# Batch 1's attention inside block 0's second product: local transposes in pairs, two score parts in one run, v spread first

## The chip, the cores and the metric

One NeuronCore of a Trainium2 chip runs the whole kernel. The metric is the device time of one execution in microseconds (us); lower is better. Engines are named as in the profile: PE (TensorE, matmuls and transposes), PEld (its weight loads), DVE (VectorE), ACT (ScalarE), POOL (GpSimd, which also issues DMAs with a cast), SP (SyncE, which issues DMAs and DMA transposes).

## What is computed

Attention of 8 batches with 8 heads (576 tokens, 64 values per head), and then a two-layer MLP over all 4608 tokens. Heads 0 to 3 look at the last 32 positions ("local"), heads 4 to 7 at every 32nd position back ("strided").

```python
scores = scale * np.matmul(q, k.transpose(0, 1, 3, 2))
mask_local = (rel >= 0) & (rel < stride)                      # stride = 32
mask_strided = (rel >= 0) & (pos[None, :] % stride == pos[:, None] % stride)
attn = softmax(np.where(mask, scores, -1e9))                  # first 4 heads local, last 4 strided
x = (attn @ v) as tokens x 512
h = x @ w_in                                                  # 512 -> 2048
out = (h * tanh(softplus(h))) @ w_out                         # 2048 -> 512
```

## The kernel before, in words

The tokens go through the MLP in 9 blocks of 512, and the attention of a batch is woven into the block before it needs it. The program's order on each engine is written by hand: `tc.manual_schedule()` keeps the order in which the Python code issues instructions, and only the waits are added (a reader waits for its writer, a buffer's next user for its last one).

Block 0 is the special one. Its second product, `mlp2` (L773 to L793), is 16 steps; each is four 128x128 by 128x512 matmuls at L781. With `fc_major=True` the steps go through the 16 chunks of w_out in four quarters: steps 0 to 3 read chunks 0 to 3, steps 4 to 7 the second quarter, steps 8 to 11 the third, steps 12 to 15 the last. Each quarter of w_out is a DMA of its own, issued on POOL's queue (L190) between the loads of batch 1's and batch 2's q, k and v. After step i the loop at L1011 runs the list `at[i]`, and these lists hold batch 1's attention. They come from `attn_steps(1, y, y)`, the branch `if x == y` (L455 to L474), in which the attention has one double PSUM bank of its own, `acc(x)`, and two single rotating banks, `tile_t` (tag "pt").

The entries of the lists, with their short names in the code:

- `T[0]` to `T[7]`, `t_step` (L245): transposes of k and q on PE into a rotating bank, and a copy to SBUF. T[0] to T[3] are the strided heads (8 transposes each, L253), T[4] to T[7] the local heads: k and q of head pair 0, then of pair 1 (12 transposes of 96x64 each, L267). The copies go to DVE (None in the list), for T[5] and T[7] to ACT.
- `Q`, `qk` (L311): score matmuls (L333) of a part, 64 rows of the array for each of two heads, into `acc(x)`, and then Exp on ACT (L347). With `"t"` for the bank it takes two rotating banks and does Exp in two instructions (L343). The strided scores have three parts (6, 6 and 4 units of two heads), the local ones too (5, 5, 2).
- `M`, `mask` (L349): a multiplication on DVE (L353).
- `V`, `pv` (L374): four matmuls (L369) into a rotating bank, then a reciprocal (L380) and a product (L381) on DVE into x_s or x_l. The first four strided pv (0 to 3) need the strided parts 0 and 1, the others parts 1 and 2.
- `spread_v_str` (L156): v of the strided heads copied on DVE from the tile in which its DMA put it to the layout that pv reads. The DMA of the next batch's v into that tile waits for it.
- `X`, `xt` (L400): transposes of the result into xT, which the MLP reads, and a copy. `xt("l", hf)` does three windows of 96 tokens of the local heads; `xt_now(n)` does n windows in one rotating bank; `xt_later(n)` leaves the windows from n on to DMA transposes on SP (L445). Later batches use the last two.
- `sums_w()` (L676): sums of quarters of w_out on DVE for the later blocks.

Before, the copies of the transposes and both parts of the first scores alternate with the steps:

```python
T[2:4], [Q(x, s0)],
[M(*s0), Q(x, s1)],
[lambda: spread_v_str(b, nc.vector), V("s", 0)],
[V("s", 1), M(*s1), Q(x, ("s", 2))],
[V("s", 2), T[4]],
[V("s", 3), M("s", 2), T[5]],
[V("s", 4), T[6]],
[V("s", 5), T[7]],
```

At L965 further work is added to the lists: at step 3 the loads of batch 2's v and local k and q on POOL (`load_early_v_str`, `load_tiles_loc`) with a cast of batch 1's local v between them, at step 12 the DMA transposes of batch 2 on SP (L224, L230), at 1, 7, 9 and 11 the sums of w_out. After step 15 block 1 begins: `mlp1(1, ...)` with its products at L553.

Of the kernel before, what the change touches and what calls it, by code (L numbers as in the profile page):

```python
# [11 lines left out]
BF16 = mybir.dt.bfloat16  # L12
# [5 lines left out]
WQ = 96  # L18
CL, PL = 6, 96
# [24 lines left out]
def kernel(ctx, tc, q, k, v, moe_w_in, moe_w_out, out):  # L44
    nc = tc.nc
# [61 lines left out]
    def acc(i, name):  # L107

        pool = ps_z[0] if i == 2 else ps_a
        return pool.tile([128, 2, 512], F32, tag=f"acc{i}", name=name)  # L110
# [23 lines left out]
    def by_head(x):  # L134

        return x[0:PL].rearrange("p j h d -> p (j h d)").rearrange("p (h x) -> p h x", h=4)
# [19 lines left out]
    def spread_v_str(b, eng):  # L156
        cast(eng, vs[b % 2][0:PN, :, :, 0:D], vs_raw().rearrange("p h (j d) -> p h j d", d=D))
# [37 lines left out]
    def cast(eng, out_, in_):  # L195
        if eng is nc.scalar:
            nc.scalar.copy(out_, in_)  # L197
        else:
            eng.tensor_copy(out_, in_)
# [42 lines left out]
            eng.memset(vl[b % 2][0:32, 0, :, 0:D], 0.0)  # L242


    def t_step(b, kind, which, hp, eng=None):  # L245

        eng = eng or nc.vector
        tr = tile_t("tr")[:].bitcast(BF16)
        if kind == "s":
            src = (qs if which == "q" else ks)[b % 2]  # L250
            for u in range(8):
                h, jj = 2 * hp + u // 4, u % 4
                nc.tensor.transpose(  # L253
                    tr[:, PN * u:PN * u + PN],
                    src[0:PN, h, 128 * jj:128 * jj + 128],
                    ident[0:PN, 0:PN],
                )
            dst = (qTs if which == "q" else kTs)[:, 8 * SU * hp:8 * SU * hp + 8 * SU]
            cast(
                eng, dst.rearrange("c (u n) -> c u n", u=8)[:, :, 0:PN],  # L260
                tr[:, 0:S].rearrange("c (u n) -> c u n", u=8),
            )
        else:
            src = by_head((ql if which == "q" else kl)[b % 2])
            for j in range(CL):
                for e in range(2):
                    nc.tensor.transpose(  # L267
                        tr[64 * e:64 * e + 64, PL * j:PL * j + PL],
                        src[:, 2 * hp + e, D * j:D * j + D], ident[0:PL, 0:PL],
                    )  # L270
            dst = qTl[:, hp, :] if which == "q" else kTl[:, hp, 32:32 + S]
            cast(
                eng, dst.rearrange("c (p j) -> c p j", j=CL),
                tr[:, 0:S].rearrange("c (j p) -> c p j", j=CL),
            )

    def unread(n, i_acc=None):

# [15 lines left out]
    class Attn:  # L294
# [129 lines left out]
                    tr[:, 0:576].rearrange("p (j n) -> p n j", j=CS),  # L424
                )

        def xt_now(self, n):
            tr = tile_t("trx")[:].bitcast(BF16)
            t0 = (self.b % RING) * S
            for c in range(2):  # L430
                for w in range(n):
                    o = (n * c + w) * WQ
                    nc.tensor.transpose(
                        tr[:, o:o + WQ], x_l[0:WQ, w, 128 * c:128 * c + 128], ident[0:WQ, 0:WQ]
                    )
            cast(
                nc.scalar, xT[:, 0:2, t0:t0 + n * WQ],
                tr[:, 0:2 * n * WQ].rearrange("p (c n) -> p c n", c=2),
            )

# [6 lines left out]
    def attn_steps(b, x, y):  # L447

        a = Attn(b)
        Q = lambda i_acc, *parts: (lambda: a.qk(parts, i_acc))  # L450
        M = lambda kd, i: (lambda: a.mask(kd, i, nc.vector))
        V = lambda kd, i: (lambda: a.pv(kd, i))
        X = lambda kd, hf: (lambda: a.xt(kd, hf))
        s0, s1, sl2, l0, l1 = ("s", 0), ("s", 1), (("s", 2), ("l", 2)), ("l", 0), ("l", 1)
        if x == y:  # L455
            T = [(lambda n=n, eng=eng: t_step(b, *T_ORDER[n], eng)) for n, eng in enumerate(
                (None, None, None, None, None, nc.scalar, None, nc.scalar))]
            return [
                T[2:4], [Q(x, s0)],
                [M(*s0), Q(x, s1)],  # L460
                [lambda: spread_v_str(b, nc.vector), V("s", 0)],
                [V("s", 1), M(*s1), Q(x, ("s", 2))],
                [V("s", 2), T[4]],
                [V("s", 3), M("s", 2), T[5]],
                [V("s", 4), T[6]],
                [V("s", 5), T[7]],
                [V("s", 6), Q(x, l0)],
                [V("s", 7), M(*l0), Q(x, l1)],
                [X("s", 0), V("l", 0), M(*l1), Q(x, ("l", 2))],
                [X("s", 1), V("l", 1), M("l", 2)],  # L470
                [V("l", 2), V("l", 3)],
                [V("l", 4), V("l", 5)],
                [lambda hf=hf: a.xt("l", hf, nc.vector) for hf in range(2)],
            ], T[0:2]  # L474
        V2 = lambda kd, i, z: (lambda: a.pv2(kd, i, z))
        G = lambda kd, i: (lambda: a.mask(kd, i, nc.gpsimd))
        l2 = ("l", 2)
        now = -(-(512 * (b + 1) - S * b) // WQ)
        at = [
            [],  # L480
            [Q(x, s0), Q(y, s1), Q("t", *sl2), M(*s0), M(*s1), M("s", 2)],
            [],
            [V2("s", 0, y), G(*l2)],
            [],
            [V2("s", 2, y), Q(x, l0), Q("t", l1), G(*l0), G(*l1)],
            [],
            [V2("s", 4, y), lambda: nc.scalar.preload_act_table(AF.Mish)],
            [],
            [V2("s", 6, y)],
            [V2("l", 0, x)],  # L490
            [X("s", 0), V2("l", 2, y), X("s", 1)],
            [V2("l", 4, x), lambda: a.xt_now(now)],
            [lambda: a.xt_later(now)],
        ]
        return at
# [364 lines left out]
    with tc.manual_schedule():  # L860
# [43 lines left out]
        a = Attn(0)  # L904
# [56 lines left out]
        for t in range(NBLK):  # L961
            if t == 0:
                x, y, z = accs
                at, ts = attn_steps(1, y, y)
                at[3] += [  # L965
                    lambda: load_early_v_str(2), lambda: load_tiles_loc(2, kl, k),
                    lambda: cast_v_loc(1, Po), lambda: load_tiles_loc(2, ql, q),
                ]
                at[12].append(lambda: transpose_by_dma(2))
                at[1].append(lambda: sums_w()[0](lo))  # L970
                at[7].append(lambda: sums_w()[0](hi))
                at[9].append(lambda: sums_w()[1](lo))
                at[11].append(lambda: sums_w()[1](hi))
                at[14].append(lambda: sums_x(1, "1"))
                at[15] += [
                    lambda: spread_v_str(2, Dv),
                ]
                out_accs = (z, x)
            else:
                if t == 1:  # L980
                    split_third()
                x, y = 0, 1
                gT, z, g1 = mlp1(t, (y, x) if t == 1 else (x, y))
                at = attn_steps(t + 1, x, y) if t + 1 < B else []
                if t == 1:
                    at[0].append(lambda: sums_w()[3](hi))
                if t + 2 < B:
                    at[10].append(lambda: transpose_by_dma(t + 2))
                if t + 1 < B:
                    at[7].append(lambda: share_v_loc(t + 1))  # L990
                if t + 2 < B:
                    at[0].append(lambda: load_qk_str(t + 2))
                if t + 1 < B:
                    at[12].append(lambda: sums_x(t + 1, "1"))
            for i, g in enumerate(g1):
                g()
                if t == 0:
                    for s in ts if i == len(g1) - 1 else ():
                        s()
                    continue  # L1000
            if t == 0:
                steps = mlp2(t, gT, out_accs, fc_major=True)
            elif t == NBLK - 1:
                mlp2_last(t, gT, z[5])
                break
            else:
                za, zc = [bank(i, "pso")[:].rearrange("p (n o) -> p n o", n=2) for i in range(2)]
                steps = mlp2_seven(t, gT, z[5], za, zc)
                if t + 1 == B:
                    steps[12] = lambda f=steps[12]: (sums_x(t + 1, "1"), f())  # L1010
            for i, g in enumerate(steps):  # L1011
                g()
                if i < len(at):
                    for s in at[i]:
                        s()
                if t > 0 and i == 9 and t + 2 < B:
                    cast_qk_loc(t + 2, Po, Po)
            if t < B - 3:
                load_qk_loc(t + 3)
# [30 lines left out]
```

## Time and profile before

| what | us |
|---|---|
| median of 3 runs | 287.12 (286.89 to 287.18) |
| the profiled execution | 286.68 |
| its span in the profile | 284.8 |
| PE busy | 279.0 (98%) |
| DVE busy | 193.0 (68%) |
| ACT busy | 196.4 (69%) |
| POOL busy | 106.3 (37%) |
| block 0's second product with batch 1's attention, PE | 35.19 to 57.39 |
| block 1, from its first matmul to that of block 2 | 57.39 to 86.44 |

The profile is of one execution, with times from the start of its span. A PE matmul's length includes the way through the pipe, so that neighbours overlap: the pace is read from the starts. Lines of one group (x12) are merged into one row of the order of time. "DMA issues" gives the time from the issue of a DMA to its landing; issue plus that time is when a waiting engine can go on.

### The profile page before, as it was taken

To read this page: it belongs to the slowest core of one execution; us is meant where nothing else is said; L and a number is where in the kernel's file an instruction comes from. 1 tells how busy PE (TensorE), PEld (TensorE's weight loads), DVE (VectorE), ACT (ScalarE), POOL (GpSimd) and SP (SyncE) were. 2 spreads that over 40 slices of the span, in tenths; PEclk is the share of its full clock that TensorE was granted. 3 is DMA by queue.
4 is the path that set the end of the run, shared out by engine and by line. 5 is a ranking of instruction groups with operands and counts; after the bars stand their busy time and mean duration, and the time that the engine had idled before them with its cause. 6 is when DMAs were issued, how large, how long until landed. Compare 5 with 4: busy or idle time off the path is not lost.

```text
span 284.8 us, 7535 instructions
## 1 busy us (share of the span) xinstructions
PE 279.0 (98%) x3121; PEld 218.6 (77%) x3121; DVE 193.0 (68%) x403; ACT 196.4 (69%) x292; POOL 106.3 (37%) x127
## 2 busy tenths in 40 slices
PE   8999999999999999999999999999999999999995
PEld 3564455586898689868988898788978997888684
DVE  2283067899877777777777778777677767644742
ACT  1578652599867987798779877987699759407820
POOL 8375534406290717271636255345404600000000
PEclk9999999999999999999999999999999999999999
DMA  7999999999989999799999999899979041003004
GB/s 155 185 202 195 190 194 201 143 145 235 169 128 129 214 173 150 139 216 158 155 138 217 122 176 136 216 135 153 157 143 164 4 154 30 0 10 140 0 2 147
DMA packets 103965, 40.73 MB, mean 143 GB/s; under 512 B 86396, under 2 KB 99436, under 8 KB 103932
## 3 DMA queue, kind: packets, MB, share of 16 engines
q1 hardware_dynamic: 67900, 25.13, 51.9%
q0 software_dynamic: 35744, 14.87, 46.8%
q8 instruction: 24, 0.39, 0.6%
q10 hardware_dynamic: 288, 0.25, 0.3%
q14 instruction: 9, 0.07, 0.1%
HBM read 37.20 MB, written 9.44 MB: 164 GB/s over the span
## 4 chain that ended last, share of the span: by engine, by line
PE 92%; DMA 2%; DVE 2%; ACT 1%; issue 0%; ACTq 0%; POOLq 0%
PE pso L748 31%; PE psu L553 10%; PE psh L522 10%; PE psv L553 9%; PE psb L553 8%; PE psb L522 5%; PE po L369 4%; PE pso L808 4%; PE pso L781 4%; PE ps L333 4%; DMA ks<-in_k_dram 2%; PE trx L418 1%; PE un L281 1%; PE tr L267 1%; PE tr L253 1%; DVE x_s L395 1%
## 5 line engine op out<-in xcount | busy, mean ns | idle before, releaser
L748 PEld LDWEIGHTS <-gT 128*128 128x128 bf16 x448 | 41.9, 98 | 5.8
L553 PEld LDWEIGHTS <-w_in 128*128 128x128 bf16 x384 | 37.4, 98 | 8.4
L353 POOL TENSOR_TENSOR Pl<-Pl,consts_sb 128x960 bf16<-128x960 bf16 (+1 forms) x18 | 29.2, 1634 | 38.2 <-issue 22.1
L748 PE MATMUL pso<-w_out,gT 128*128 128x256 bf16 x336 | 40.9, 272 | 0.0
L748 PEld LDWEIGHTS <-Sg 128*128 128x128 bf16 x336 | 31.5, 98 | 4.4
L522 PEld LDWEIGHTS <-w_in 128*128 128x128 bf16 x208 | 20.2, 98 | 16.7 <-issue 0.6
L553 PEld LDWEIGHTS <-Sw 128*128 128x128 bf16 x288 | 28.2, 98 | 3.3
L522 PE MATMUL psh<-xT,w_in 128*128 128x512 bf16 (+1 forms) x136 | 29.4, 366 | 0.2 <-ACT xT L197 0.2
L197 ACT COPY xT<-trx 128x576 bf16<-128x576 bf16 (+3 forms) x24 | 14.2, 629 | 18.4 <-PE trx L418 13.0
L748 PE MATMUL pso<-Tw,Sg 128*128 128x256 bf16 x224 | 26.7, 273 | 0.0
L197 ACT COPY osb<-pso 128x512 f32<-128x512 f32 (+1 forms) x17 | 9.4, 555 | 20.2 <-PE pso L748 10.8
L562 ACT ACTIVATE gT<-psu 128x1024 bf16<-128x1024 f32 x16 | 16.4, 1025 | 8.4 <-PE psu L553 8.4
L395 DVE TENSOR_TENSOR x_s<-po,rden 72x512 bf16<-72x512 f32 x28 | 19.2, 686 | 1.0
L656 DVE TENSOR_TENSOR psu<-psb,p 128x512 f32<-128x512 f32 x16 | 11.2, 700 | 11.8 <-PE psb L553 11.0
L533 ACT ACTIVATE gT<-psh 128x1024 bf16<-128x1024 f32 x16 | 16.2, 1024 | 4.0 <-PE psh L522 3.9
L175 POOL DMA_DIRECT2D vl<-in_v_dram x24 | 17.8, 751 | 2.0 <-issue 1.5
L656 DVE TENSOR_TENSOR Sg<-gT 128x256 bf16<-128x256 bf16 (+2 forms) x32 | 12.8, 422 | 8.0 <-ACT gT L562 6.7
L628 POOL COPY mark<-qTl 1x4 bf16<-1x4 bf16 x6 | 1.6, 268 | 44.4 <-DMA qTl<-ql 44.4
L347 ACT ACTIVATE Ps<-ps 72x864 bf16<-72x864 f32 (+1 forms) x18 | 14.7, 857 | 4.6 <-PE ps L333 4.6
L553 PE MATMUL psu<-xT,w_in 128*128 128x256 bf16 x128 | 17.9, 272 | 0.0
L725 DVE TENSOR_TENSOR p<-pso,p 128x512 f32<-128x512 f32 x14 | 9.6, 685 | 11.9 <-PE pso L748 11.9
L553 PE MATMUL psb<-Sx,w_in 128*128 128x256 bf16 x128 | 17.2, 272 | 0.0
(139 smaller groups left out, 612.8 us busy)
## 6 DMA issues: line engine op xcount, KB each, us to landing
out_dram<-osb SPq DMA_DIRECT2D x9, 512.0 KB, 3.9
out_dram<-p SPq DMA_DIRECT2D x7, 512.0 KB, 3.0
kl<-in_k_dram SPq DMA_DIRECT2D x5, 576.0 KB, 13.6
ql<-in_q_dram SPq DMA_DIRECT2D x5, 576.0 KB, 16.4
qs<-in_q_dram POOLq DMA_DIRECT2D x8, 288.0 KB, 12.0
vsr<-in_v_dram POOLq DMA_DIRECT2D x8, 288.0 KB, 9.0
w_in<-in_moe_w_in_dram POOLq DMA_DIRECT2D x4, 512.0 KB, 9.8
w_out<-in_moe_w_out_dram POOLq DMA_DIRECT2D x4, 512.0 KB, 17.9
```

Of the source, the lines that this page charges most:

```text
L175: nc.gpsimd.dma_start(vl[b % 2][32:128, :, h, 0:D], v[b, h].rearrange("(w p) d -> p w d", p=WQ))
L197: nc.scalar.copy(out_, in_)
L333: nc.tensor.matmul(by_e[e][:, o:o + w], lhsT=lhsT, rhs=rhs, start=not biased, stop=True, skip_group_check=biased,)
L347: nc.scalar.activation(pt[0:n, :, 0:nw], ps[0:n, :, o0:o0 + nw], AF.Exp, scale=scale)
L353: meng.tensor_tensor(out=pm, in0=pm, in1=mk[0:n, :].unsqueeze(1).unsqueeze(1).to_broadcast([n, 2, nu, w]), op=ALU.mult,)
L395: nc.vector.tensor_tensor(out=dst.rearrange("p e (h d) -> p e h d", h=4), in0=po[0:m, :, :, 0:D], in1=rden[0:m].unsqueeze(3).to_broadcast( ...
L522: nc.tensor.matmul(ps_u[:, o:o + n], lhsT=w_in[:, cc, fc * 128:(fc + 1) * 128], rhs=xT[:, cc, a:a + n], start=(cc == 2 and (o == 0 or len( ...
L533: nc.scalar.activation(to, tiles[g][:], AF.Mish)
L553: nc.tensor.matmul(p[:, 256 * j:256 * j + 256], lhsT=lhs[:, cc, f:f + 128], rhs=rhs[:, cc], start=(first and j == 0 and cc == 0), stop=(la ...
L562: nc.scalar.activation(gT[:, c:c + src.shape[1], 256 * half_t:256 * half_t + 256], src, AF.Mish,)
L656: nc.vector.tensor_tensor(out=out_, in0=in0, in1=in1, op=op)
L748: nc.tensor.matmul(ps[:, pair, :], lhsT=lhs(c, 128 * pair), rhs=rhs(c), start=(first and pair == 0 and c == 0), stop=(last and c == 7), sk ...
```

## The change

It concerns `attn_steps` for batch 1 alone (and moves one sum).

- The local transposes of both head pairs are done in one run of 24 into the two halves of `acc(x)`, k after step 5 and q after step 7, and then copied: pair 0 on DVE, pair 1 on ACT. T[4] to T[7] at steps 5 to 8 are gone. The transposes of `t_step` become a function, `t_loc`, which returns the copy.
- The strided score parts 0 and 1 are done in one run after step 1; part 1 goes to the two rotating banks, its Exp in two instructions.
- v is spread on DVE ahead of the masks, after step 1 and not after step 3; both masks follow. The mask of part 2 comes right behind the pv of step 5.
- The local heads' result goes to xT with `xt_now(5)` on DVE (10 transposes and one copy) and a DMA transpose of the sixth window, where two `xt` of six transposes were.
- The first half of the first sum of w_out moves from the list of step 1 to that of step 0.

```diff
+    def t_loc(b, which, hp, tr):
+        src = by_head((ql if which == "q" else kl)[b % 2])
+        for j in range(CL):
+            for e in range(2):
+                nc.tensor.transpose(
+                    tr[64 * e:64 * e + 64, PL * j:PL * j + PL],
+                    src[:, 2 * hp + e, D * j:D * j + D], ident[0:PL, 0:PL],
+                )
+        dst = qTl[:, hp, :] if which == "q" else kTl[:, hp, 32:32 + S]
+        return lambda eng: cast(
+            eng, dst.rearrange("c (p j) -> c p j", j=CL),
+            tr[:, 0:S].rearrange("c (j p) -> c p j", j=CL),
+        )
...
-        def xt_now(self, n):
+        def xt_now(self, n, eng=nc.scalar):
...
-            T = [(lambda n=n, eng=eng: t_step(b, *T_ORDER[n], eng)) for n, eng in enumerate(
-                (None, None, None, None, None, nc.scalar, None, nc.scalar))]
+            T = [(lambda n=n: t_step(b, *T_ORDER[n])) for n in range(4)]
+
+            def t_pair(which):
+                tr = acc(x, "tr")
+                copies = [t_loc(b, which, hp, tr[:, hp, :].bitcast(BF16)) for hp in range(2)]
+                for copy, eng in zip(copies, (nc.vector, nc.scalar)):
+                    copy(eng)
+
             return [
-                T[2:4], [Q(x, s0)],
-                [M(*s0), Q(x, s1)],
-                [lambda: spread_v_str(b, nc.vector), V("s", 0)],
-                [V("s", 1), M(*s1), Q(x, ("s", 2))],
-                [V("s", 2), T[4]],
-                [V("s", 3), M("s", 2), T[5]],
-                [V("s", 4), T[6]],
-                [V("s", 5), T[7]],
+                T[2:4],
+                [Q(x, s0), Q("t", s1), lambda: spread_v_str(b, nc.vector), M(*s0), M(*s1)],
+                [],
+                [V("s", 0)],
+                [V("s", 1), Q(x, ("s", 2))],
+                [V("s", 2), M("s", 2), lambda: t_pair("k")],
+                [V("s", 3)],
+                [V("s", 4), lambda: t_pair("q")],
+                [V("s", 5)],
                 [V("s", 6), Q(x, l0)],
                 [V("s", 7), M(*l0), Q(x, l1)],
...
-                [lambda hf=hf: a.xt("l", hf, nc.vector) for hf in range(2)],
+                [lambda: a.xt_now(5, nc.vector), lambda: a.xt_later(5)],
             ], T[0:2]
...
-                at[1].append(lambda: sums_w()[0](lo))
+                at[0].append(lambda: sums_w()[0](lo))
```

More of the change, by code (lines that the diff above doesn't have):

```diff
@@ L263, in t_step @@
         else:
[L264 to L275, printed above, removed]
+            t_loc(b, which, hp, tr)(eng)
     def unread(n, i_acc=None):
@@ L436, in xt_now @@
             cast(
-                nc.scalar, xT[:, 0:2, t0:t0 + n * WQ],
+                eng, xT[:, 0:2, t0:t0 + n * WQ],
                 tr[:, 0:2 * n * WQ].rearrange("p (c n) -> p c n", c=2),
```

## The prediction, as it was put on record

> **What bounds the kernel now.** I read the page's first and fourth parts, then the order of time for TensorE in the one stage that the change touches (35 to 58 us), then for the engines that feed it, then the landings of the DMAs issued before it.
>
> The page's chain that ended last, shares by engine:
>
> ```profile
> PE 92%; DMA 2%; DVE 2%; ACT 1%; issue 0%; ACTq 0%; POOLq 0%
> ```
>
> So a microsecond is saved only where TensorE gets one less to do or to wait for. The stage is block 0's second product, 16 steps of four L781 matmuls, with batch 1's attention put between them. From the order of time for PE (start, length, what; the length includes the pipe, so I go by starts):
>
> ```profile
> 36.58 1.03 PE L781 MATMUL pso<-w_out,gT 128*128 128x512 bf16 x4
> 37.54 0.37 PE L333 MATMUL ps<-qTs,kTs 64*128 64x72 bf16 x12
> 37.84 1.04 PE L781 MATMUL pso<-w_out,gT 128*128 128x512 bf16 x4
> 38.95 0.37 PE L333 MATMUL ps<-qTs,kTs 64*128 64x72 bf16 x12
> 39.25 1.04 PE L781 MATMUL pso<-w_out,gT 128*128 128x512 bf16 x4
> ...
> 44.12 0.29 PE L369 MATMUL po<-vs,Ps 72*128 72x65 bf16 x4
> 44.34 0.45 PE L267 MATMUL tr<-consts_sb,Sg 96*64 96x96 bf16 x12
> 44.72 1.04 PE L781 MATMUL pso<-w_out,gT 128*128 128x512 bf16 x4
> 45.59 0.28 PE L369 MATMUL po<-vs,Ps 72*128 72x65 bf16 x4
> 45.81 0.45 PE L267 MATMUL tr<-consts_sb,Sg 96*64 96x96 bf16 x12
> 46.25 1.02 PE L781 MATMUL pso<-w_out,gT 128*128 128x512 bf16 x4
> 47.11 0.29 PE L369 MATMUL po<-vs,Ps 72*128 72x65 bf16 x4
> 47.33 0.45 PE L267 MATMUL tr<-consts_sb,Sg 96*64 96x96 bf16 x12
> 47.71 1.04 PE L781 MATMUL pso<-w_out,gT 128*128 128x512 bf16 x4
> 48.58 0.29 PE L369 MATMUL po<-vs,Ps 72*128 72x65 bf16 x4
> 48.80 0.39 PE L333 MATMUL ps<-qTl,kTl 64*128 64x96 bf16 x10
> ```
>
> A step is 0.87 us (47.71 to 48.58). A pv of four matmuls is 0.12 before a step (40.19 to 40.31) and 0.22 before a run that uses half the array, scores or local transposes (44.12 to 44.34). Twelve local transposes take 0.38 (44.34 to 44.72), but their starts, 0.45 less the 0.21 of one, spread over 0.24: 0.022 each, and some 0.12 pass between the last and the next step. So each run on half the array costs about 0.09 to enter and 0.12 to leave, whatever its length. (The Trainium skill, TensorEngine Tiling (Array Packing), Tiling Modes, says that a change of the tiling mode, not merely of the tile, drains TensorE; these gaps agree.)
>
> In this order there is one step that waits for a DMA. Step 8 (46.25) is the first that reads the third quarter of w_out (chunks 8 to 11). Its load, in the order of time for POOL and in the DMA issues of that moment:
>
> ```profile
> 25.88 0.76 POOL L190 DMA_DIRECT2D w_out<-in_moe_w_out_dram  x1 [1.26 <-DMA w_in<-in_moe_w_in_dram]
> ```
> ```profile
> w_out<-in_moe_w_out_dram POOLq DMA_DIRECT2D x1, 512.0 KB, 20.3
> ```
>
> 25.88 + 20.3 = 46.18. The transposes ahead of step 8 take 0.44 until it starts, all others 0.38: TensorE was ready at 46.19 and began at 46.25. Step 8 sits on that landing already.
>
> **The change, part by part,** in TensorE's time up to step 8, then behind it.
>
> Both first score parts in one run. Before, the second waits at 38.71 until Exp has emptied the first one's banks (Exp 38.01 to 38.90), and starts at 38.95. After, it uses the two rotating banks and follows at once: 24 matmuls at 0.0166 (block 1 runs 32 of them from 71.97 to 72.50, 0.53) plus 0.10 to leave, 0.50, so step 2 starts at 38.04 and step 3 ends at 39.78. Its Exp becomes two instructions of 72x432: the rows beside it are 406 ns for 72x288 and 571 for 128x480; I take 0.52, nearer the larger. They end near 39.95; the first pv's bank is free at 39.44.
>
> v spread ahead of the masks. DVE does it while it waits for Exp (37.94 to 38.93 idle; 0.68), the first mask still ends at 39.53, before the pv at 39.78. Before, that pv waited for the spread (39.46 + 0.68 = 40.14, pv 40.19). What hides it is that idle time; without it the spread would cost up to 0.68 there. It also frees v's raw tile at about 38.6 and not 40.14, so POOL issues the next v load and the first local k load some 1.6 us sooner (rival 3). The second mask (0.59) now stands ahead of the first pv's DVE work, until 40.55; behind it wait only that pv's two instructions (0.6), and nobody needs their bank before 42.09.
>
> The w_out sum moved from step 1 to step 0 stays where it is on DVE, behind the last q copy at 37.26: nothing.
>
> Transposes in pairs. 24 in one run: between 0.64 (0.38 + 12 x 0.022) and 0.76 (twice 0.38); I take 0.64, by the starts. In the built program both copies wait for all 24, and ACT's copy waits for DVE's, one behind the other: 0.74 (DVE, kTl) + 0.64 (ACT). For k: DVE is free at 43.5, ACT ends at 44.9; the q run, which reuses the banks, comes at 45.03. For q they end at 47.3, the local scores come at 48.33. Cover 0.1 and 1.0; a delay of the first falls into the wait for step 8 below and costs nothing up to 0.6.
>
> Sum to step 8: 38.04, two steps 39.78, pv 39.90, step 40.77, pv 40.99, third scores 0.23 to 41.22, step 42.09, pv 42.31, k run 42.95, step 43.82, pv 43.94, step 44.81, pv 45.03, q run 45.67. TensorE is 0.52 earlier though the last 12 transposes already lie behind it. But the quarter of w_out lands at 46.18, so step 8 starts at 46.25 as before and **0.58 us become a new wait**.
>
> Behind step 8: before 46.25 to 48.80 (two steps, two pv, 12 transposes, the local scores next). After: 0.87 + 0.12 + 0.87 + 0.22, so 48.33. **Gain 0.47** = 0.38 of transposes + 0.10 of a pv that no longer leads into half the array. From here the order is the old one, shifted. The last quarter of w_out (29.75 + 20.2 = 49.95) is due at step 12, 51.71; the local v on POOL, ready at 50.04, at 51.29. Neither binds.
>
> The end: ten transposes for twelve, 12 take 0.52 (56.87 to 57.39), so 0.09 less, **gain 0.09**. Its bound: block 1's second product waits for ACT's copy of the stage's last banks, 1.01 behind the last step, and has 0.05 left after the change. One DVE copy of 128x960 for two of 128x576: bounds 0.41 (one) and 0.82 (both, 57.33 on); 0.68 by length, done before TensorE needs it at 59.1. The sixth window goes by a DMA transpose on SP, ahead of batch 3's k and q loads (65.30, 66.36). Block 1's row for two of these holds SP 3.49, so 1.2 to 1.8 for one; q lands at 83.16, up to 85 after; POOL casts it at 83.70 in 1.6, and SP reads it at 88.61. Hidden by 2 us; xT's own window is due in block 2, 86.
>
> **Sum: 0.47 + 0.09 = 0.56 us.** The profiled execution took 286.68 (span 284.8 and 1.88 around it), so 286.12; the median of the runs is 287.12, 0.44 higher, and I take the difference from it: **286.56**, -0.195%. A measurement of this kernel tells about 0.2% (0.57 us) from no change.
>
> **Rivals.**
> 1. The quarter of w_out lands sooner than in the profiled execution. Then step 8 starts at 46.19 before and as early as 45.67 after: 0.52 + 0.47 + 0.09 = 1.08, 286.04. Nothing in the change quickens it; the DMA row of the page is full at that time, so that a run's landings may shift by some tenths.
> 2. Runs on half the array have no fixed price, and the gaps belong to single instructions. Then a pair costs 0.76, TensorE reaches step 8 at about 46.2 anyway, and behind it only 0.38 + 0.09 = 0.47 go: 286.65. The 32 scores of block 1 in one run speak against it.
> 3. Slower: the v load issued 1.6 us sooner takes bandwidth from the quarter of w_out. It takes 1.3 us of the queue (qs lands at 52.9, vsr at 54.2); if all of that went ahead of w_out, step 8 would start 1.3 late: 1.3 - 0.56 = +0.74, 287.86. It decides from 0.56 us of delay on. Against it: the loads of POOL's queue land in the order of their issue (w_out 38.1, k 41.0, q 43.0, w_out 46.2, w_out 50.0, ks 51.9, qs 52.9, vsr 54.2), and this one is issued behind five that land before it. (The Trainium skill, DMA: Bandwidth & Descriptors, Issuing engines are not separate DMA queues, has the DMAs of all engines interleave on the same 16, and the section after it says that those of one engine are not ordered; that speaks for this rival, the landings here against it.)
> 4. The pairs don't shorten anything, since a wait for ACT's second copy takes their place: a delay over 0.6 at the q run. It would need DVE to be half a microsecond later than above; then the gain shrinks toward 0, 287.1.
>
> **How the numbers follow.** Forecast 0.60 (by itself 286.3 to 286.85, small terms and noise); rival 1 0.14, rival 2 0.10, rival 3 0.10, rival 4 0.06. Range 285.9 to 287.4: it takes in rivals 1, 2 and 4 and the lower half of 3. The forecast lies on the 0.2% line, so I split it 0.50 same and 0.50 faster, 0.30 each; rival 1 goes to faster, 2 and 4 to same, and rival 3 0.08 to slower, 0.02 to same: faster 0.44, same 0.48, slower 0.08.
>
> **What would show it.** In the profile after: the 24 strided scores from 37.54 in one group of about 0.5; step 8 still at 46.2 to 46.3 with 0.5 to 0.6 of idle TensorE just before it, no attention work in it; the first local scores near 48.3; block 1 starting near 56.8 and not 57.39, and every later block moved by the same. I am wrong if w_out's third quarter lands at another time (1, 3), if a pair takes 0.76 (2), if TensorE waits ahead of the q run (4), or if a later block gives the gain back at a wait for a DMA.

## The result, and the profile after

The changed kernel takes 286.31 us (median of 21 runs, 285.50 to 286.84) where the kernel before takes 286.92 (21 runs, 286.64 to 287.52). The ratio of the runs is 0.9971, 95% interval 0.9965 to 0.9978: faster by 0.29% of 286.92, which is 0.83 us, 0.63 to 1.00. (The two medians are 0.61 us apart, which by themselves would be a ratio of 0.9979.) Forecast were 0.56 us as the likeliest and 1.08 for rival 1; what was measured lies between them.

The profiled execution after took 286.66 us, as good as the one before (286.68), and its span is the same 284.8. The gain is there all the same, but this execution began the stage 0.41 us later: step 0 starts at 35.60 where it started at 35.19, and TensorE is 0.39 us late at 8.40 already, where it waits for a load of batch 0's k (8.01 before), far ahead of any changed instruction. So two profiles are compared stage by stage here. The order of time for PE in the changed stage (start, length, what; in brackets the idle time in front, and what ended it):

```profile
37.95 0.56 PE L336 MATMUL ps<-qTs,kTs 64*128 64x72 bf16 x24
38.45 1.90 PE L791 MATMUL pso<-w_out,gT 128*128 128x512 bf16 x8
...
42.72 0.70 PE L249 MATMUL tr<-consts_sb,Sg 96*64 96x96 bf16 x24
43.35 1.04 PE L791 MATMUL pso<-w_out,gT 128*128 128x512 bf16 x4
...
45.43 0.70 PE L249 MATMUL tr<-consts_sb,Sg 96*64 96x96 bf16 x24
46.68 1.02 PE L791 MATMUL pso<-w_out,gT 128*128 128x512 bf16 x3 [0.55 <-DMA w_out<-in_moe_w_out_dram]
47.54 0.29 PE L372 MATMUL po<-vs,Ps 72*128 72x65 bf16 x4
47.66 1.03 PE L791 MATMUL pso<-w_out,gT 128*128 128x512 bf16 x4
48.53 0.28 PE L372 MATMUL po<-vs,Ps 72*128 72x65 bf16 x4
48.74 0.39 PE L336 MATMUL ps<-qTl,kTl 64*128 64x96 bf16 x10
...
57.25 1.04 PE L563 MATMUL psu<-xT,w_in 128*128 128x256 bf16 x8
```

The new wait stands in the sixth of these lines: TensorE is done with the second run of transposes and sits idle until a part of w_out has landed. From step 0 to block 1 the stage takes 57.25 - 35.60 = 21.65 us, and 57.39 - 35.19 = 22.20 before: 0.55 less.

The chain that ended last, by engine, shows the same on the page. Before it ran through TensorE at 92%; now, followed back from the end, it turns off at that wait into the loads:

```profile
PE 81%; DMA 14%; POOL 2%; DVE 1%; issue 1%; ACT 0%; POOLq 0%
```

And the start of that chain in order of time, from 20 us on (start, length, what):

```profile
17.37 8.49 DMA w_in<-in_moe_w_in_dram
25.86 0.28 issue
26.14 20.50 DMA w_out<-in_moe_w_out_dram
46.64 0.04 issue
46.68 0.38 PE pso L791
```

The issue of that load in the order of time for POOL, and its row among the DMA issues:

```profile
26.14 0.76 POOL L190 DMA_DIRECT2D w_out<-in_moe_w_out_dram  x1 [1.17 <-DMA w_in<-in_moe_w_in_dram]
```
```profile
w_out<-in_moe_w_out_dram POOLq DMA_DIRECT2D x1, 512.0 KB, 20.5
```

POOL waits for a load of w_in until 25.86, issues the third quarter of w_out at 26.14, and the quarter lands 20.5 us later, at 46.64. In this execution a shorter TensorE program ahead of 46.64 can't move anything behind it.

### The profile page after: what moved, and what is told of

Its sections match the earlier page's. It is cut to its first block, busy times and chain, and to the rows that moved or that the text cites. A ratio compares the mean times of both kernels' runs of the same rounds, so it can differ in the third digit from the quotient of the medians.

```text
span 284.8 us, 7519 instructions
## 1 busy us (share of the span) xinstructions
PE 277.2 (97%) x3105; PEld 218.2 (77%) x3119; DVE 195.8 (69%) x402; ACT 196.2 (69%) x293; POOL 108.0 (38%) x127
## 4 chain that ended last, share of the span: by engine, by line
PE 81%; DMA 14%; POOL 2%; DVE 1%; issue 1%; ACT 0%; POOLq 0%
PE pso L758 31%; PE psu L563 10%; PE psv L563 9%; PE psb L563 8%; DMA w_out<-in_moe_w_out_dram 7%; PE psb L532 5%; PE psh L532 5%; PE pso L818 4%; PE po L372 4%; DMA vl<-in_v_dram 3%; DMA w_in<-in_moe_w_in_dram 3%; PE ps L336 3%; PE pso L791 2%; PE trx L421 1%; PE trx L436 1%
## 5 line engine op out<-in xcount | busy, mean ns | idle before, releaser
L350 ACT ACTIVATE Ps<-ps 72x864 bf16<-72x864 f32 (+1 forms) x17 | 13.8, 854 | 4.2 <-PE ps L336 4.2
```

Source lines behind the costliest of these rows:

```text
L350: nc.scalar.activation(pt[0:n, :, 0:nw], ps[0:n, :, o0:o0 + nw], AF.Exp, scale=scale)
```

## The experiments

The stage in the profiled execution of each, from step 0 to block 1, is the cleanest measure, since the rest hardly changes (span less start of block 1: 227.4 to 227.8 in all of them). "Ready" is the time from step 0 to the end of what stands ahead of step 8, by the starts and the lengths of the runs.

| kernel | step 0 | ready after | step 8 | block 1 | stage | time, against before on the same chip |
|---|---|---|---|---|---|---|
| before | 35.19 | 11.00 | 46.25 | 57.39 | 22.20 | |
| after | 35.60 | 10.46 | 46.68 | 57.25 | 21.65 | 286.31, 286.92 |
| e1 pairs | 35.34 | 11.03 | 46.37 | 57.78 | 22.44 | 286.48, 286.88 |
| e2 scores | 35.44 | 10.43 | 46.80 | 57.94 | 22.50 | 287.05, 286.88 |
| e3 xT | 34.98 | 11.00 | 45.98 | 57.05 | 22.07 | 286.88, 286.88 |
| e4 after | 35.41 | 10.46 | 46.61 | 57.18 | 21.77 | 286.39, 286.88 |
| e5 before, half v | 35.62 | 11.00 | 46.62 | 57.77 | 22.15 | 286.82, 286.88 |
| e6 after, half v | 35.70 | 10.46 | 46.16 | 56.75 | 21.05 | 285.64, 286.88 |
| e7 fill | 35.50 | | 46.38 | 56.71 | 21.21 | 285.90, 286.88 |
| e8 after | 35.41 | 10.45 | 46.35 | 56.92 | 21.51 | 285.82, 286.88 |
| e9 before, split | 35.36 | 10.99 | 46.35 | 57.50 | 22.14 | 286.81, 286.90 |
| e10 scores, split | 35.04 | 10.43 | 45.47 | 56.62 | 21.58 | 286.45, 286.90 |
| e11 after, split | 35.26 | 10.46 | 45.72 | 56.30 | 21.04 | 285.63, 286.90 |
| e12 after | 35.12 | 10.46 | 46.10 | 56.67 | 21.55 | 286.16, 286.90 |

**The parts alone.** e1, the pairs of transposes (with the old score order, xT and sums):

```diff
-                [V("s", 2), T[4]],
-                [V("s", 3), M("s", 2), T[5]],
-                [V("s", 4), T[6]],
-                [V("s", 5), T[7]],
+                [V("s", 2), M("s", 2), lambda: t_pair("k")],
+                [V("s", 3)],
+                [V("s", 4), lambda: t_pair("q")],
+                [V("s", 5)],
```

> The pairs of local transposes alone, the rest as before. Theory (a wait for the third quarter of w_out ahead of step 8): TensorE reaches step 8 at about 46.2, just as the quarter lands, so there is hardly a wait, and behind step 8 the whole 0.47 us is gained: -0.47 us (-0.16%). In its profile two runs of 24 transposes of about 0.64 each, the step behind the second at the landing. Rival (runs on half the array have no price of their own): runs of 0.76 and -0.38 us.

Measured: ratio 0.9992, 0.9983 to 1.0001: between no change and the 0.47 us expected, and the median is 0.40 below. Its profile has the expected shape at step 8 (ready at 46.37, no wait). But it has another wait that was foreseen only as a margin of 1.3 us: the first local pv waits for POOL, which casts batch 1's local v only when that has landed, at 49.4 in this execution. The order of time for POOL and PE:

```profile
49.43 2.42 POOL L199 CAST vl<-vl 128x768 bf16<-128x768 f32 x2 [2.44 <-DMA vl<-in_v_dram]
51.80 0.30 POOL L242 MEMSET vl<- 32x256 bf16 x1
```
```profile
52.16 0.29 PE L372 MATMUL po<-vl,Pl 128*128 128x65 bf16 x4 [0.57 <-POOL vl L242]
```

Step 8 to block 1 takes 57.78 - 46.37 = 11.41 here and 11.14 before. The pv stood ready behind the transposes of x_s, 0.26 after 51.16, so 0.74 are this wait, and without it the part is 11.41 - 0.74 - 11.14 = -0.47, as expected. Its eleven runs fall into two groups, seven at 286.22 to 286.51 and four, the profiled one among them, at 287.01 to 287.31. The two are about as far apart as this wait is long, which suggests, but doesn't show, that a kernel that gets there sooner meets this landing in some executions and not in others.

e2, the score run, v spread first, masks and the sum:

```diff
-                T[2:4], [Q(x, s0)],
-                [M(*s0), Q(x, s1)],
-                [lambda: spread_v_str(b, nc.vector), V("s", 0)],
-                [V("s", 1), M(*s1), Q(x, ("s", 2))],
+                T[2:4],
+                [Q(x, s0), Q("t", s1), lambda: spread_v_str(b, nc.vector), M(*s0), M(*s1)],
+                [],
+                [V("s", 0)],
+                [V("s", 1), Q(x, ("s", 2))],
```

> The two score parts in one run, v spread first, the masks behind it and the sum moved; transposes one by one and xT as before. Theory: TensorE is 0.56 us earlier at step 8 (45.63 against 46.19) and loses what the landing of w_out's third quarter takes. If that quarter lands as late as in the profile of before (20.3 us behind its issue), the gain is 0 and the profile shows a wait of some 0.6 us right ahead of step 8; rival 1 (it lands sooner in most executions) gives up to -0.56 us (-0.2%). Rival 3 (the v load issued sooner delays w_out) gives a quarter that lands later than 20.5 us behind its issue, and a time above that of before.

Measured: ratio 1.0003, 0.9992 to 1.0015, no gain. TensorE is ready 0.57 sooner than before (10.43 against 11.00) and loses all of it; the waits of PE from 44 to 47.5 us name the place (total, times, longest):

```profile
PE pso L782 <- DMA w_out<-in_moe_w_out_dram: 0.9, 1, 0.9
```

Its quarter of w_out lands 20.6 us behind its issue. The median hides a wide spread, though: of the twelve runs three are 0.45 to 0.54 below the median of before, which would fit an early landing (rival 1), and five are 0.56 to 0.85 above it.

Rival 3 (the v load, issued sooner, slows w_out) stays open in a smaller size. With the v load late, the quarter takes 20.3 us (before), 19.3 (e1) and 19.0 (e3) from its issue; with the v load early, 20.5 (after), 20.6 (e2, e4), 19.9 (e7), 20.4 (e8) and 19.5 (e12). The means are 0.7 us apart and the two sets overlap. With half of the local v or with the split load (both below) the difference is gone: 18.1 late against 17.6 early, and 19.0 late against 19.3 and 18.1 early for the first half. So 1.3 us, the size that the rival was given, isn't seen; some tenths are neither shown nor excluded. No run has the score run with the v load left late, which would tell.

e3, ten transposes, one copy and a DMA transpose:

```diff
-                [lambda hf=hf: a.xt("l", hf, nc.vector) for hf in range(2)],
+                [lambda: a.xt_now(5, nc.vector), lambda: a.xt_later(5)],
```

> Ten transposes and one copy for the local result, and the sixth window by a DMA transpose; the rest as before. Theory: -0.09 us, all on TensorE at the end of the stage, too little to be told from no change. Rival: the DMA transpose on SP delays the loads of batch 3 and something later waits: then slower, and a wait for a DMA in blocks 1 or 2.

Measured: ratio 1.0001, 0.9992 to 1.0010, as expected too little to see; in the profile the stage is 0.13 shorter, 0.06 of it because TensorE didn't wait at step 8. The rival (something later waits because of the DMA transpose) doesn't show: from 33 us to the end no wait of TensorE for a DMA is in its profile.

e4, the whole change beside its parts:

> The changed kernel itself, beside its parts and on the same chip: -0.6 to -0.8 us. If the parts add up, it is the sum of the three others; by the theory pairs and scores together can't give more than the landing of w_out's third quarter lets through, 0.47 us when it lands late and 1.0 when it lands before TensorE gets there.

Measured: ratio 0.9978, 0.9970 to 0.9987, so 0.37 to 0.86 us faster. The parts' medians (-0.40, +0.17, 0.00) sum to less than the whole (-0.49), though their intervals are too wide to hold that against the sum.

**The wait taken away, by less traffic.** Half of batch 1's local v isn't loaded, before (e5) and after (e6):

```diff
-        load_v_loc(1)
+        first = v[1, 2:3, 0:1, :].offset - 32 * D
+        nc.sync.dma_start(heads[:, 12:24, :], bass.AP(v.tensor, first, [[D, 128], [WQ * D, 12], [1, D]]))
```

> The kernel before, with half of batch 1's local v (the load on SP's queue of 0.77 MB) left out: heads 2 and 3 are loaded, heads 0 and 1 keep batch 0's values. The transfers that run beside w_out's third quarter are 0.38 MB less, so that it lands some 1 to 2 us sooner. Theory: before, TensorE reaches step 8 just as the quarter lands in the profiled execution, so this alone gives only what other executions waited there, 0 to -0.3 us.

> The changed kernel with the same half of batch 1's local v left out. Theory: the wait ahead of step 8 is gone, and the whole change shows: 0.52 + 0.47 + 0.09 = 1.08 us below the same cut of the kernel before. Rival (the wait ahead of step 8 isn't for the quarter of w_out, or the price of the parts is wrong): the difference between the two cuts stays at 0.6 to 0.8.

Measured: e5 0.9996 (0.9987 to 1.0006), e6 0.9950 (0.9932 to 0.9969, five runs). Now the quarter lands 18.1 and 17.6 us behind its issue. Between the two cuts lie 286.82 - 285.64 = 1.18 us, and 22.15 - 21.05 = 1.10 in the profiles; 1.08 was expected. Step 8 follows the second run of transposes at once:

```profile
45.53 0.70 PE L249 MATMUL tr<-consts_sb,Sg 96*64 96x96 bf16 x24
46.16 1.04 PE L791 MATMUL pso<-w_out,gT 128*128 128x512 bf16 x3
```

The kernel before gains nothing from the same cut: it came to step 8 just when the quarter had landed. The cut also brings the local v itself sooner: it is ready on POOL at 47.99 and 46.65, where before it was at 50.04. So the runs of e6 alone don't tell a wait for w_out from one for the local v. The last four runs below do, since they leave the local v as it is.

**The wait filled with other work.** Two pv go ahead of step 8:

```diff
-                [V("s", 4), lambda: t_pair("q")],
-                [V("s", 5)],
-                [V("s", 6), Q(x, l0)],
+                [V("s", 4), lambda: t_pair("q"), V("s", 5), V("s", 6)],
+                [],
+                [Q(x, l0)],
```

> The changed kernel with the strided pv 5 and 6 moved from behind steps 8 and 9 to ahead of step 8, into the wait. Theory: each takes 0.12 us off the time behind step 8 where the wait is long enough, -0.24 us against the changed kernel when the quarter of w_out lands as late as in the profile, 0 when it lands early, so some -0.1 to -0.2 us against it, -0.8 to -1.0 against before. Rival: DVE, with two more pv in a row, gives the buffers back late, and the pv wait: then no gain, and idle TensorE ahead of the pv.

> The changed kernel once more, beside these three: -0.6 to -0.8 us against before; the landing of w_out's third quarter in its profile 20 to 20.7 us behind its issue.

Measured: e7 0.9966 (0.9955 to 0.9977), e8 0.9956 (0.9938 to 0.9974). In the profile the two pv stand in the wait:

```profile
45.33 0.70 PE L249 MATMUL tr<-consts_sb,Sg 96*64 96x96 bf16 x24
45.96 0.46 PE L372 MATMUL po<-vs,Ps 72*128 72x65 bf16 x8
46.38 1.89 PE L791 MATMUL pso<-w_out,gT 128*128 128x512 bf16 x7
```

From step 8 to block 1 they save 10.57 - 10.33 = 0.24, as expected, and no idle TensorE stands ahead of them, so that the rival (late buffers) doesn't show. The times don't show it: 285.90 against 285.82 for the changed kernel on the same chip. There the changed kernel was faster than elsewhere (1.06 below before by the medians, outside the 0.6 to 0.8 expected of e8), as if the quarter landed early in most executions; in its profile it landed late, with a wait of 0.42. Inconclusive as a gain.

**The wait taken away with nothing left out.** The third quarter is loaded in two halves, and steps 8 and 9 take the first half for all four output tiles, 10 and 11 the second:

```diff
-        def group(ot, g4):
+        def group(ot, g4, fcs=None):
...
-            for fc in range(4 * g4, 4 * g4 + 4):
+            for fc in fcs or range(4 * g4, 4 * g4 + 4):
...
-        return [lambda o=o: group(*o) for o in order]
+        steps = [lambda o=o: group(*o) for o in order]
+        for n in range(4):
+            fcs, ots = range(8 + 2 * (n // 2), 10 + 2 * (n // 2)), (2 * (n % 2), 2 * (n % 2) + 1)
+            steps[8 + n] = lambda fcs=fcs, ots=ots: [group(ot, 2, fcs) for ot in ots]
+        return steps
...
-        load_w_out(2, 4)
+        for c0 in (8, 10):
+            nc.gpsimd.dma_start(
+                w_out[:, c0:c0 + 2, :],
+                moe_w_out.rearrange("(fc p) o -> p fc o", p=128)[:, c0:c0 + 2, :],
+            )
+        load_w_out(3, 4)
```

> The kernel before, with the third quarter of w_out loaded in two DMAs of two chunks, and steps 8 to 11 in the order of these halves (steps 8 and 9 take chunks 8 and 9 of all four output tiles, 10 and 11 take chunks 10 and 11), so that what step 8 needs lands some 1.6 us sooner. Nothing is left out. Theory: before, TensorE comes to step 8 just as the quarter lands, so 0 to -0.1 us.

> The score run, early spread and masks alone, on the same split load. Theory: the 0.56 us that this part gains ahead of step 8 were lost at the landing; with the split they show: -0.5 us, of which the local v (its cast on POOL ready between 49.5 and 52, needed 0.56 sooner than before) may take some back. Rival (the score run gains nothing on TensorE): 0 as without the split.

> The changed kernel on the same split load. Theory: the wait ahead of step 8 is gone, up to -1.1 us against before, which is -0.3 to -0.5 against the changed kernel beside it; the local pv 0 then comes 1.0 us sooner than before, at about 50.7, and where POOL's cast of the local v ends later, as in some profiles, a wait there takes part of it back: then -0.7 to -0.9, with a wait for POOL ahead of the first local pv. Rival (another thing than the load holds step 8): as the changed kernel.

> The changed kernel beside these: -0.6 to -1.0 us against before, the wait for w_out ahead of step 8 again in its profile.

Measured: e9 0.9990 (0.9980 to 1.0000), e10 0.9981 (0.9971 to 0.9991), e11 0.9953 (0.9936 to 0.9971), e12 0.9974 (0.9960 to 0.9987). The score part, worth nothing on the old load, shows on the split one: e10 is 0.26 to 0.83 us below before, and 0.36 below e9, which has the split load alone (medians of twelve runs each). The stages add up: 22.14 with neither, 21.58 with the scores (-0.56), 21.04 with the whole change (-1.10). In all three the first half has landed when TensorE is ready for step 8: at 44.89, 45.10 and 43.81, against 46.35, 45.47 and 45.72. The issue of the first half in e11, 18.1 us ahead of its landing, and then the order of time for PE:

```profile
25.71 0.71 POOL L953 DMA_DIRECT2D w_out<-in_moe_w_out_dram  x1 [1.36 <-DMA w_in<-in_moe_w_in_dram]
```

```profile
45.09 0.70 PE L249 MATMUL tr<-consts_sb,Sg 96*64 96x96 bf16 x24
45.72 1.04 PE L791 MATMUL pso<-w_out,gT 128*128 128x512 bf16 x3
46.60 0.29 PE L372 MATMUL po<-vs,Ps 72*128 72x65 bf16 x4
...
56.30 1.04 PE L563 MATMUL psu<-xT,w_in 128*128 128x256 bf16 x8
```

e11 is the best version here: 285.63, 0.53 us below the changed kernel beside it and 1.27 below before by the medians. Its runs are only six, but all are at or below 286.09, and seven of the twelve of e12 lie above that. The wait for POOL that was feared at the first local pv isn't in its profile (the local v was ready at 48.9, needed at 50.76).

## Why the prediction was right, point by point

- **TensorE is the bound, and step 8 sits on a landing.** Right, and it decided the result. Ready after 10.46 was measured, 10.48 had been worked out (45.67 - 35.19); the wait was put at 0.58, and the profiled executions after had 0.55, 0.67, 0.42 and 0.45 by their rows (after, e4, e8, e12). e2 against e10 shows that it takes a real gain away. With the later start of 0.41 taken off, the first local scores (48.74) and block 1 (57.25) come at 48.33 and 56.84, as foreseen. That the fit is so close is partly luck, since the quarter happened to land 0.46 later in the profile after than in the one before: the four profiled stages of the changed kernel are 0.43 to 0.69 shorter than the one before.
- **A run on half the array has a price to enter and to leave.** Right. A pair of transposes takes 42.72 to 43.35, 0.63, where twice 0.38 stood before; 0.64 had been taken. The 24 scores take 0.50, as worked out. Rival 2 falls. (The Trainium skill, TensorEngine Tiling (Array Packing), Tiling Modes, has a change of the tiling mode drain TensorE; these numbers agree.)
- **Behind step 8: 0.47.** Measured in the profile: 46.68 to 48.74 is 2.06, and 46.25 to 48.80 is 2.55: 0.49.
- **The end: 0.09.** Ten transposes take 56.82 to 57.25, 0.43 for 0.52. The copy of 128x960 took 0.66 (0.68 taken). The runs are too noisy to show this part by itself (e3).
- **The copies one behind the other.** Right: ACT's copy of k starts at 44.53, behind DVE's (43.75 and 0.75 long), and ends at 45.17; the q run at 45.43 wasn't held. Rival 4 falls.
- **"Neither binds", the last quarter and the local v.** It held in the four profiles of the changed kernel, though in two with little room (after: local v ready at 51.01, first local pv at 51.71; e4: 50.95 and 51.64). It failed in e1's, with a wait of 0.74 that the prediction had no rival for.
- **The DMA transpose on SP.** Its price was too small, 2.30 us on SP and not 1.2 to 1.8. Batch 3's q is cast at 85.36 instead of 83.70, and SP reads it at 88.80 instead of 88.61. Still hidden, by 1.56 and not by 2 us: the cast is done at 87.24.
- **The size: 0.83 measured, 0.56 forecast.** The step that fell short is "step 8 starts at 46.25 as before": it was taken from one execution as a fixed time. Step 8 starts at the later of two things, TensorE's own work and the landing, and only the landing was allowed to decide. The runs' spread fits this: before they lie within 0.88 us, after within 1.34; the highest times of each are 0.68 apart (287.52 and 286.84), near the forecast, and the lowest 1.14 (286.64 and 285.50), near rival 1, where e6 and e11 lie too. That the quarter lands early in the executions with the lowest times is inferred, since no profile of the changed kernel caught one; the split load shows what an early landing is worth. How much of the spread is the local v's doing isn't shown either; it is unlikely to be most of it, since e11 leaves the local v as it is and its six runs lie within 0.57 us. The early landing was given a chance of 0.14 as a rival of its own, when it is the other end of one range.
- **The chances.** "Same" had 0.48 and "faster" 0.44, since the forecast lay on the line of 0.57 us that the prediction took as the least to be told from no change. It came out faster, by a little more than that line. The forecast left this to a coin toss and said so.

## What to carry to other kernels

Ahead of a time at which a transfer lands, count where the engine would be without it: work saved there gains nothing once the engine arrives before the load does, and work moved from behind the landing into the wait is worth its full length as long as the wait lasts (0.24 in the stage of e7, though not in its times). When a change shows less than its parts should give, look in the chain of waits for a load that has newly entered it; loading what is needed first as a transfer of its own (here a quarter in two halves) can release a gain that is already paid for. And short runs that use the array in another shape are best made few and long: each cost about 0.2 us here, to enter and to leave, beside the work itself.

## What had not been expected of the hardware

Two profiled executions of one program, or of two that are alike up to there, enter this stage up to 0.7 us apart (34.98 to 35.70), and the same load, with the whole local v beside it, lands 19.0 to 20.6 us behind its issue, which itself comes at 25.88 to 26.56. POOL's cast of the same local v took 1.59 us in eight of the fourteen profiles, 1.66 in e7, 1.81 in e11 and 2.05 to 2.42 in e10, after, e4 and e1. What makes it longer there is left open. All three are of the size of the gain in question, so that one profile of each kernel, read as a whole, shows no difference here (284.8 and 284.8), and the stages show it.
